# Attention and spectral mix on one core: other cuts of q over the DMA engines

## The chip, the core and the metric

The kernel runs on one core of a Trainium2 chip. A core has TensorE (PE; its weight loads are shown apart, as PEld), VectorE (DVE), ScalarE (ACT), GpSimd (POOL) and SyncE (SP). Sixteen DMA engines move data between memory (HBM) and the core's own memory of 128 partitions. POOL and SP issue the transfers; POOL's go through queue 0 and change float32 into bfloat16 on the way, SP's through queue 1.

The metric is the time of one execution on the device in microseconds (us), the median of several runs.

## The reference

Sliding-window causal attention over 8 batches, 8 heads, 576 positions and 64 channels, then a mix in the frequency domain with one complex 512 x 512 matrix for each of 64 modes, then a channel product:

```python
def _attn_ref(q, k, v):                     # q, k, v: (8, 8, 576, 64) float32
    scores = scale * np.matmul(q, k.transpose(0, 1, 3, 2))
    mask = (rel >= 0) & (rel < 64)          # rel = query position - key position
    ...
    return np.matmul(attn, v)

def _moe_ref(x, w_r, w_i, w_ch):            # x: (8, 576, 512), the heads side by side
    X = np.fft.rfft(x, axis=1)              # w_r, w_i: (64, 512, 512), w_ch: (512, 512)
    Yr = einsum("bmd,mde->bme", Xr, w_r) - einsum("bmd,mde->bme", Xi, w_i)
    Yi = einsum("bmd,mde->bme", Xr, w_i) + einsum("bmd,mde->bme", Xi, w_r)
    Y[:, :n_modes] = Yr + 1j * Yi
    u = x + np.fft.irfft(Y, n=S, axis=1)
    return u + np.maximum(u @ w_ch, 0.0)
```

Most of the bytes are weights: 127 matrices of 512 x 512 float32 (w_i of mode 0 isn't needed) make 133 of the 162.5 MB that are read.

## The kernel before, in words

**Stages.** Lines 465 to 543 are attention. Batch by batch, PE transposes k, v and q (`transpose_units`, line 275, with the transposes at line 289), forms the scores in windows of 512 columns (line 361), ACT takes the exponential (line 367), PE multiplies with v (line 385), DVE normalises into `x_sb` (line 393), and PE does the forward transform (line 407). The next stage, lines 947 to 976, runs over the 127 weights in a fixed order: `half` (line 652) multiplies one weight with the transformed rows (line 660), `issue` (line 609) starts the loads of later weights as places come free, and pieces of the channel product and the inverse transform are set between them. The end (from line 1039) has the products that need the last modes, and writes the output through SP (lines 1031 and 1034).

**Loads.** POOL issues, in the order of the program, q, k and v of each batch (`load`, line 137) and the weights (`load_w`, line 177, one of 512 KB in bfloat16; `load_two`, line 182, two in one transfer). The order of PE and POOL is written out by hand (`manual_schedule`); DVE's and ACT's is not in the attention stage. `refill` (line 444) is called after each unit of transposes: once k of batch b has been transposed, it loads k of batch b + 2 into the same buffer (two buffers of each kind, `rawp`) and then, from batch 1 on, one weight (`early`, line 428); the same with v and q. So the loads of batch 5 are issued while batch 3 is in work, those of batch 7 while batch 5 is.

Each transfer of POOL ends on one of eight semaphores, which go round: the ninth transfer waits until the first has landed on all its engines.

**How rows go to DMA engines.** A tensor of a batch is 128 partitions by two halves (heads 0 to 3 and 4 to 7) of 18 x 64 values, 2304 bytes in bfloat16. Transferred whole (line 152) it gives each of the sixteen engines 16 such rows. Three loads of q, those of batches 5, 6 and 7, are cut by `UNEVEN` (line 113). An entry is (n, m, columns, small one behind): the first n x m partitions of the lower half are read as n groups interleaved (line 143, outer dimension n), which puts them on n engines alone, m rows on each. These are n engines in turn, from where the last such transfer stopped; for the entry with 17, one engine. The upper half (line 145) goes over all sixteen, 8 rows each. What is left of the lower half (line 148: 3, 72 and 94 rows) goes in equal parts from engine 0 on. `step_on` (line 131) issues a small transfer of 2n rows of 32 bytes that nobody reads: it moves the turn on by n engines. The assertion of line 116 keeps the sum of all turns a multiple of 16.

| batch | turn | rows of the cut, each | small one behind |
| --- | --- | --- | --- |
| 5 | engines 0 to 4 | 25 | 5, 6 |
| 6 | engines 7, 8 | 28 | 9 to 14 |
| 7 | engine 15 | 34 | none |

**The order is undone in the transposes.** The interleaved rows stand in other partitions. `back` (line 121) makes for each cut a permuted identity (two DVE copies, lines 126 and 127), and `part` (line 283) takes it in place of `ident_bf` for the half that was cut (line 291).

Of the kernel before, what the change touches and what calls it, by code (L numbers as in the profile page):

```python
# [11 lines left out]
BF16 = mybir.dt.bfloat16  # L12
# [8 lines left out]
def view(ap, off, dims):  # L21

    return bass.AP(ap.tensor, ap.offset + off, [list(ap.ap[0])] + [list(d) for d in dims])
# [3 lines left out]
def kernel(  # L27
# [10 lines left out]
    nc = tc.nc  # L38
    B, H, S, D = q.shape
# [8 lines left out]
    RUN = S // 32  # L48
# [6 lines left out]
    def evac(o, i, on_act):  # L55

        if on_act:
            return nc.scalar.copy(out=o, in_=i)  # L58
        return nc.vector.tensor_copy(out=o, in_=i)  # L59
# [10 lines left out]
    ident_bf = consts.tile([128, 128], BF16, name="ident_bf")  # L70
# [19 lines left out]
    acons = p1.enter_context(tc.tile_pool(name="acons", bufs=1, side="right"))  # L90
# [10 lines left out]
    RAW = {"k": k, "q": q, "v": v}  # L101

    def raw_tile(which):
        return rawp.tile([128, 2, RUN * D], BF16, name="r" + which)

    def runs(b, which):
        return RAW[which][b].rearrange("(x g) (p c) d -> (g p) x (c d)", g=4, c=RUN)
# [1 line left out]

    UNEVEN = {(5, "q"): (5, 25, RUN, 2), (6, "q"): (2, 28, RUN, 6), (7, "q"): (17, 2, RUN, 0)}
    for lot in UNEVEN.values():
        assert lot[0] <= 16 or all(lot[0] % d for d in range(2, 17))
    assert sum((n if n <= 16 else 1) + x for n, m, c, x in UNEVEN.values()) % 16 == 0
    aside = [acons.tile([34, 16], BF16, name=f"aside{i}") for i in range(len(UNEVEN))]
    forms = {lot[:2]: acons.tile([128, 128], BF16, name=f"back{lot[0]}") for lot in UNEVEN.values()}
    made = set()

    def back(key):

        n, m = form = UNEVEN[key][:2]
        if form not in made:
            made.add(form)
            nc.vector.tensor_copy(out=forms[form], in_=ident_bf)
            nc.vector.tensor_copy(out=view(forms[form], 0, [[1, n], [n, m]]),
                                  in_=view(ident_bf, 0, [[m, n], [1, m]]))
        return forms[form]

    def step_on(key, n):

        n, src = (n if n > 1 else 17), k[0, :H // 2].rearrange("g (p c) d -> (g p) (c d)", c=RUN)
        nc.gpsimd.dma_start(out=aside[list(UNEVEN).index(key)][:2 * n],
                            in_=src[:2 * n, 0:16].rearrange("(r a) c -> a r c", a=n))

    def load(b, which):
        r = raw_tile(which)
        if (b, which) in UNEVEN:
            lower, upper = [RAW[which][b, x * H // 2:(x + 1) * H // 2].rearrange("g (p c) d -> (g p) (c d)", c=RUN)  # L140
                            for x in range(2)]
            n, m, c, behind = UNEVEN[b, which]
            cut = lower[:n * m].rearrange("(r a) c -> a r c", a=n)
            nc.gpsimd.dma_start(out=r[:n * m, 0, :c * D], in_=cut[:, :, :c * D])
            nc.gpsimd.dma_start(out=r[:, 1, :], in_=upper)
            if c < RUN:
                nc.gpsimd.dma_start(out=r[:, 0, c * D:], in_=lower[:, c * D:])
            nc.gpsimd.dma_start(out=r[n * m:, 0, :c * D], in_=lower[n * m:, :c * D])
            if behind:
                step_on((b, which), behind)  # L150
        else:
            nc.gpsimd.dma_start(out=r, in_=runs(b, which))
        raws[b, which] = r
# [65 lines left out]
    with tc.manual_schedule(engines=ALL_FOUR):  # L219
# [3 lines left out]
        with tc.tile_pool(name="tmpf", bufs=1, side="right") as tmp:  # L223
            mo = tmp.tile([128, NM], FP32, name="mo")
            to = tmp.tile([128, NT], FP32, name="to")
            nc.gpsimd.iota(mo, pattern=[[1, NM]], base=0, channel_multiplier=0,
                           allow_small_or_imprecise_dtypes=True)
            nc.gpsimd.iota(to, pattern=[[128, NT]], base=0, channel_multiplier=1,
                           allow_small_or_imprecise_dtypes=True)
            nc.gpsimd.memset(ident, 0.0)  # L230
            nc.gpsimd.affine_select(out=ident, in_=ident, compare_op=ALU.not_equal, fill=1.0,
                                    base=0, pattern=[[-1, 128]], channel_multiplier=1)
            load(0, "q")
            load(0, "v")
            for t0, t1 in ((0, 3), (3, NT)):
                n = t1 - t0
                mt = tmp.tile([128, 2, n * NM], FP32, name="mtf")
                nc.vector.tensor_tensor(out=view(mt, 0, [[NM, n], [1, NM]]), in0=view(mo, 0, [[0, n], [1, NM]]),
                                        in1=view(to, t0, [[1, n], [0, NM]]), op=ALU.mult)
                gen_trig(tmp, mt, n * NM, trigF[:, t0:t1, 0:NM], trigF[:, t0:t1, NM:2 * NM], "f")  # L240
                if t0 == 0:
                    nc.vector.tensor_copy(out=ident_bf, in_=ident)
        nc.scalar.activation(out=spark, in_=ident[:, 0:1], func=ACT_F.Exp)
        raws[0, "k"] = raw_tile("k")
        for c, engine in enumerate((nc.vector, nc.gpsimd, nc.vector)):
            cc = slice(6 * D * c, 6 * D * (c + 1))
            engine.tensor_copy(out=raws[0, "k"][:, :, cc], in_=k_first[:, :, cc])
        load(1, "k")
        for i in range(4):
            half = i % 2  # L250
# [24 lines left out]
    def transpose_units(b):  # L275

        rk, rq, rv = (raws.pop((b, which)) for which in "kqv")
        qT = qtp.tile([128, 4, S], BF16, name="qT")
        vT = vtp.tile([128, 4, S], BF16, name="vT")
        kT, vt = kTs[b % 2], vts[b % 2]  # L280
        qTs[b] = qT

        def part(src, dst, c0, on_act, which):
            def f():
                turned = UNEVEN.get((b, which), (0, 0, 0))[2]
                ps = ps_misc.tile([128, 6, 128], BF16, name="pst", tag="misc")
                for c in range(6):
                    for hh in range(2):
                        nc.tensor.transpose(out=ps[64 * hh:64 * hh + 64, c, :],  # L289
                                            in_=src[:, hh, (c0 + c) * D:(c0 + c + 1) * D],  # L290
                                            identity=back((b, which)) if hh == 0 and c0 + c < turned else ident_bf)
                evac(view(dst, c0, [[S, 4], [RUN, 32], [1, 6]]),
                     view(ps, 0, [[32, 4], [1, 32], [128, 6]]), on_act)
            return f

        def vback(u):
            def f():
                ps = ps_misc.tile([128, 6, 128], BF16, name="psv", tag="misc")
                for i in range(6):
                    a, j = divmod(6 * u + i, 9)  # L300
                    if j == 4:
                        parts = [(0, 64, 2 * a, 512), (64, 64, 2 * a + 1, 0)]
                    else:
                        parts = [(0, 128, 2 * a + (j > 4), 128 * j - (j > 4) * S)]
                    for r0, n, g, t0 in parts:
                        nc.tensor.transpose(out=ps[r0:r0 + n, i, :],  # L306
                                            in_=vT[:, g, t0:t0 + n], identity=ident_bf)
                evac(view(vt, 6 * u * VW, [[18 * VW, 2], [VW, 6], [1, D]]),
                     view(ps, 0, [[D, 2], [128, 6], [1, D]]), u != 1)
                if u:  # L310
                    hs = slice(u - 1, u + 2, 2)
                    nc.vector.tensor_copy(out=vt[64:128, 1, hs, 1:9], in_=vt[64:128, 0, hs, 0:8])
                    nc.vector.tensor_copy(out=vt[0:64, 1, hs], in_=vt[0:64, 0, hs])
            return f

        return [*(part(rk, kT, 6 * i, i != 1, "k") for i in range(3)),
                *(part(rv, vT, 6 * i, i == 1, "v") for i in range(3)),
                *(part(rq, qT, 6 * i, i != 1, "q") for i in range(3)),
                vback(0), vback(1), vback(2)]
# [50 lines left out]
    def closes(w):  # L370

        return min(-(-8 * w // 9) * 9 or 9, 8 * w + 8)
# [115 lines left out]
    with tc.manual_schedule(engines={E.PE, E.Pool}):  # L488
# [16 lines left out]
        for w in range(NWIN + 1):  # L505
# [5 lines left out]
            n = len(todo)  # L511
            if 0 < w < NWIN:
                scores(w)
            if w:
                cut = closes(w - 1)
# [12 lines left out]
            if w in (NWIN - 4, NWIN - 1):  # L528
                i = (B - 2) % 2 if w == NWIN - 4 else (B - 1) % 2
                spare(kTs[i])  # L530
                spare(qtp.tile([128, 4, S], BF16, name="qT"))
            if w in (NWIN - 4, NWIN):
                i = (B - 2) % 2 if w == NWIN - 4 else (B - 1) % 2
# [386 lines left out]
    for k, (f, delta, n, few) in enumerate(items):  # L920
        i = S_I + k * (T_I - 2 - S_I) // len(items)
# [25 lines left out]
    with tc.manual_schedule(engines=ALL_FOUR):  # L947
# [92 lines left out]
        for k in range(6):  # L1040
# [10 lines left out]
                              in_=view(psys[0], 0, [[2 * B, NC], [2, B], [1, 2]]))  # L1051
# [78 lines left out]
```

## Time and profile before

Three runs: 423.84, 423.85 and 424.44 us; median 423.85.

| what | us |
| --- | --- |
| the profiled execution | 424.01 |
| its span, first to last instruction | 422.2 |
| PE busy | 350.5 |
| DVE busy | 189.9 |
| ACT busy | 159.9 |
| POOL busy | 86.5 |
| mean granted clock of TensorE | 0.859 of full |

HBM is read at 162.53 MB and written at 9.44 MB. The page gives bytes of a transfer as they arrive: 92.55 MB over 31312 packets, since POOL's loads halve the bytes. In the page's rows a line such as `wt<-in_moe_w_i_dram POOLq DMA_DIRECT2D x19, 512.0 KB, 15.8` tells of 19 transfers of 512 KB that took 15.8 us (median) from issue to landing. In a timeline the columns are start, duration, engine, line, operation and tiles, number merged, and in brackets the idle time before it with what ended it.

### The profile page before, as it was taken

Reading aid. Unit: us, or ns where it says so; the run is one execution under the profiler, and the core shown is the slowest. Engines: PE = TensorE matmul, PEld = TensorE weight load, DVE = VectorE, ACT = ScalarE, POOL = GpSimd, SP = SyncE. Lnnn points to the kernel's source line nnn. Section 1 sums busy time; section 2 is a strip of 40 time slices with the busy share of each in tenths; the row PEclk is TensorE's granted clock in tenths of the full one; section 3 lists DMA queues with packets and bytes.
Section 4 is the critical chain, followed back from the end, with each engine's and each line's share of the span. In section 5 each row is a group of like instructions: output and inputs, shape, how many; then the busy total and the mean of one; then the engine's idle time right before and its main releaser. Section 6 shows DMA issues by size and latency. Waiting matters only on the chain.

```text
span 422.2 us, 11483 instructions
## 1 busy us (share of the span) xinstructions
PE 350.5 (83%) x5185; PEld 230.8 (55%) x5185; DVE 189.9 (45%) x365; ACT 159.9 (38%) x267; POOL 86.5 (20%) x154
## 2 busy tenths in 40 slices
PE   7899999999988779954768576767699999998994
PEld 3466666656654566743546454545456565554441
DVE  6576776676764100634343251211114344340895
ACT  5666865766765100122102110200023343330863
POOL 6231232341221220411112011210121212300000
PEclk9999999999999655978668665667579999999998
DMA  8999999999999999999999999999999999997598
GB/s 211 212 213 213 214 212 209 213 209 209 213 215 213 213 214 262 214 214 215 214 213 215 213 215 213 215 214 214 214 214 215 213 214 213 214 215 144 208 371 318
DMA packets 31312, 92.55 MB, mean 219 GB/s; under 512 B 3744, under 2 KB 3744, under 8 KB 31264
## 3 DMA queue, kind: packets, MB, share of 16 engines
q0 software_dynamic: 26016, 81.21, 96.5%
q1 hardware_dynamic: 5248, 10.62, 6.9%
q8 instruction: 40, 0.66, 0.6%
q14 instruction: 8, 0.07, 0.0%
HBM read 162.53 MB, written 9.44 MB: 407 GB/s over the span
## 4 chain that ended last, share of the span: by engine, by line
DMA 44%; PE 40%; DVE 7%; issue 3%; ACT 2%; DVEq 0%; POOLq 0%; ACTq 0%
DMA wms<-in_moe_w_i_dram 23%; DMA wms<-in_moe_w_r_dram 22%; PE psy L660 6%; PE pso L385 6%; PE pst L289 5%; PE psv L306 3%; PE psx L407 3%; PE pss L1005 3%; DVE x_sb L393 2%; PE pss L998 2%; PE pss L342 2%; PE pss L361 2%; PE psz L801 2%; PE psy L945 2%; DVE vT L59 1%
## 5 line engine op out<-in xcount | busy, mean ns | idle before, releaser
L801 PE MATMUL psz<-wch,xT 128*128 128x512 f32 x144 | 59.2, 548 | 0.0
L795 DVE CAST xT<-pxt 128x1024 fp32r<-128x1024 bf16 x18 | 22.0, 1224 | 78.5 <-PE pxt L790 78.5
L804 ACT CAST Z<-psz 128x1024 fp32r<-128x1024 f32 x18 | 18.2, 1012 | 99.0 <-PE psz L801 99.0
L367 ACT ACTIVATE et<-pss 128x512 bf16<-128x512 f32 x72 | 39.2, 600 | 13.6 <-PE pss L361 13.6
L660 PE MATMUL psy<-XQ,wls 128*128 128x16 bf16 x560 | 21.9, 192 | 23.8 <-DMA wls<-in_moe_w_r_dram 15.1
L660 PE MATMUL psy<-XQ,wms 128*128 128x16 bf16 x624 | 25.1, 192 | 19.9 <-DMA wms<-in_moe_w_i_dram 13.8
L660 PEld LDWEIGHTS <-wms 128*128 128x128 bf16 x624 | 21.4, 102 | 31.9 <-DMA wms<-in_moe_w_i_dram 16.7
L660 PEld LDWEIGHTS <-wls 128*128 128x128 bf16 x560 | 19.3, 104 | 33.4 <-DMA wls<-in_moe_w_r_dram 18.2
L801 PEld LDWEIGHTS psz<-wch,xT 128*128 128x128 f32 x144 | 33.8, 261 | 5.2
L385 PE MATMUL pso<-vt,et 128*64 128x65 bf16 (+1 forms) x576 | 32.3, 203 | 4.3 <-DVE x_sb L393 1.9
L853 DVE TENSOR_TENSOR Z<-pse,Z 128x1024 fp32r<-128x1024 f32 x16 | 19.6, 1225 | 29.7 <-PE pse L842 29.7
L385 PEld LDWEIGHTS <-et 128*64 128x64 bf16 (+1 forms) x576 | 22.2, 109 | 15.1 <-issue 7.7
L660 PE MATMUL psy<-XQ,wt 128*128 128x16 bf16 x560 | 20.9, 192 | 7.1 <-issue 3.0
L393 DVE TENSOR_TENSOR x_sb<-pso,rcp 128x640 bf16<-128x640 f32 x32 | 26.3, 822 | 0.9
L660 PEld LDWEIGHTS <-wt 128*128 128x128 bf16 x560 | 18.5, 105 | 11.7 <-DMA wt<-in_moe_w_i_dram 4.5
L59 DVE COPY vT<-pst 128x768 bf16<-128x768 bf16 x16 | 15.3, 958 | 13.1 <-PE pst L289 11.6
L1023 ACT ACTIVATE pss<-pss 128x512 f32<-128x512 f32 x35 | 18.5, 581 | 4.8 <-PE pss L1005 4.2
L59 DVE CAST YT<-psy 128x256 fp32r<-128x256 f32 x6 | 2.5, 424 | 38.6 <-PE psy L660 29.6
L945 PE MATMUL psy<-trigF,ident_bf 128*128 128x512 bf16 x46 | 17.6, 447 | 0.1
L58 ACT COPY vt<-psv 128x768 bf16<-128x768 bf16 x16 | 12.9, 809 | 8.3 <-PE psv L306 8.2
L306 PE MATMUL psv<-ident_bf,vT 128*128 128x128 bf16 (+1 forms) x160 | 15.5, 226 | 0.6 <-DVE vT L59 0.6
L342 PE MATMUL pss<-band,ident_bf 64*64 64x512 bf16 x120 | 15.9, 397 | 0.0
(198 smaller groups left out, 621.8 us busy)
## 6 DMA issues: line engine op xcount, KB each, us to landing
wt<-in_moe_w_i_dram POOLq DMA_DIRECT2D x19, 512.0 KB, 15.8
wt<-in_moe_w_r_dram POOLq DMA_DIRECT2D x16, 512.0 KB, 16.7
wls<-in_moe_w_r_dram POOLq DMA_DIRECT2D x8, 1024.0 KB, 21.6
wms<-in_moe_w_i_dram POOLq DMA_DIRECT2D x7, 1024.0 KB, 21.2
wms<-in_moe_w_r_dram POOLq DMA_DIRECT2D x7, 1024.0 KB, 21.2
wls<-in_moe_w_i_dram POOLq DMA_DIRECT2D x6, 1024.0 KB, 21.6
rv<-in_v_dram POOLq DMA_DIRECT2D x8, 576.0 KB, 12.8
rk<-in_k_dram POOLq DMA_DIRECT2D x7, 576.0 KB, 12.4
```

Of the source, the lines that this page charges most:

```text
L59: return nc.vector.tensor_copy(out=o, in_=i)
L289: nc.tensor.transpose(out=ps[64 * hh:64 * hh + 64, c, :], in_=src[:, hh, (c0 + c) * D:(c0 + c + 1) * D], identity=back((b, which)) if hh = ...
L306: nc.tensor.transpose(out=ps[r0:r0 + n, i, :], in_=vT[:, g, t0:t0 + n], identity=ident_bf)
L342: nc.tensor.matmul(out=pss[(2 * w + hh) % 3][64 * half:64 * half + 64, :], lhsT=ident_bf[pp, pp], rhs=view(band[pp], 128 * half, [[0, WIN ...
L367: nc.scalar.activation(out=et[:, hh, :], in_=pss[(2 * w + hh) % 3], func=ACT_F.Exp, scale=EX_SCALE)
L385: nc.tensor.matmul(out=pso[po, hh, block(b, i // 2) * VW:block(b, i // 2) * VW + D + 1], lhsT=et[pk, hh, col:col + 64], rhs=vt[pk, 1 - f % ...
L393: nc.vector.tensor_tensor(out=view(x_sb, b * NT * DM + g * D, [[4 * D, 2], [DM, NT], [1, D]]), in0=view(pso, 0, [[512, 2], [VW, NT], [1, D]]),
L660: nc.tensor.matmul(out=view(psy, off + 2 * B * e, [[1, 2 * B]]), lhsT=w[:, c, 128 * e:128 * e + 128], rhs=XQ[:, m // HM, c, :, 1 - im:3 - ...
L795: nc.vector.tensor_copy(out=o, in_=i)
L801: nc.tensor.matmul(out=psz[s][:, j, :], lhsT=xts[s % 2][0][:, j, 128 * c:128 * c + 128], rhs=wch[:, c, :], start=(c == 0), stop=(c == NC - 1))
L853: nc.vector.tensor_tensor(out=z, in0=ps, in1=z, op=ALU.add)
L945: nc.tensor.matmul(out=o, lhsT=ident_bf, rhs=view(trigF, 0, [[1, DM]]), start=True, stop=True)
```

## The change

It concerns the loads of k and q of batches 5, 6 and 7. The eight engines that get more rows than the others are the same: 0 to 4, 7, 8 and 15.

- q of batch 5 is cut with (2, 32, 1): 64 partitions of the lower half as two groups of 32, then the upper half over all sixteen engines, then the other 64 partitions of the lower half.
- q of batch 6 is cut with (6, 16, 2): 96 partitions of the lower half as six groups of 16, a small transfer for ten engines, 96 partitions of the upper half as six groups of 16, then the last 32 partitions of both halves.
- q of batch 7 is loaded whole.
- Small transfers (`lead_on`) for 7, 6 and 11 engines are issued ahead of k of batches 5, 6 and 7 (`STEPS`); none follow q.
- `back` is built for two cuts where there were three, and `part` takes it for as many halves as were cut.

The turns are then:

| before | transfer | engines | rows each |
| --- | --- | --- | --- |
| k of 5 | small, 7 | 0 to 6 | small |
| in q of 5 | cut of 2 | 7, 8 | 32 |
| k of 6 | small, 6 | 9 to 14 | small |
| in q of 6 | cut of 6 | 15, 0 to 4 | 16 |
| in q of 6 | small, 10 | 5 to 14 | small |
| in q of 6 | cut of 6 | 15, 0 to 4 | 16 |
| k of 7 | small, 11 | 5 to 15 | small |

POOL issues 131 transfers before and after.

```diff
-    UNEVEN = {(5, "q"): (5, 25, RUN, 2), (6, "q"): (2, 28, RUN, 6), (7, "q"): (17, 2, RUN, 0)}
...
-    aside = [acons.tile([34, 16], BF16, name=f"aside{i}") for i in range(len(UNEVEN))]
+    UNEVEN = {(5, "q"): (2, 32, 1), (6, "q"): (6, 16, 2)}
+    STEPS = {(5, "k"): 7, (6, "k"): 6, (7, "k"): 11}
+    assert (sum(STEPS.values()) + sum((n, n + 16)[i - 1] for n, m, i in UNEVEN.values())) % 16 == 0
...
-    def step_on(key, n):
-
-        n, src = (n if n > 1 else 17), k[0, :H // 2].rearrange("g (p c) d -> (g p) (c d)", c=RUN)
-        nc.gpsimd.dma_start(out=aside[list(UNEVEN).index(key)][:2 * n],
-                            in_=src[:2 * n, 0:16].rearrange("(r a) c -> a r c", a=n))
+    def raw_rows(b, which, x):
+        return RAW[which][b, x * H // 2:(x + 1) * H // 2].rearrange("g (p c) d -> (g p) (c d)", c=RUN)
+
+    def lead_on(n):
+        aside = acons.tile([2 * n, 16], BF16, name=f"aside{n}")
+        nc.gpsimd.dma_start(out=aside, in_=raw_rows(0, "k", 0)[:2 * n, 0:16].rearrange("(r a) c -> a r c", a=n))

     def load(b, which):
+        if (b, which) in STEPS:
+            lead_on(STEPS[b, which])
         r = raw_tile(which)
         if (b, which) in UNEVEN:
...
-            n, m, c, behind = UNEVEN[b, which]
-            cut = lower[:n * m].rearrange("(r a) c -> a r c", a=n)
-            nc.gpsimd.dma_start(out=r[:n * m, 0, :c * D], in_=cut[:, :, :c * D])
-            nc.gpsimd.dma_start(out=r[:, 1, :], in_=upper)
-            if c < RUN:
-                nc.gpsimd.dma_start(out=r[:, 0, c * D:], in_=lower[:, c * D:])
-            nc.gpsimd.dma_start(out=r[n * m:, 0, :c * D], in_=lower[n * m:, :c * D])
-            if behind:
-                step_on((b, which), behind)
+            n, m, halves = UNEVEN[b, which]
+            for x in range(halves):
+                nc.gpsimd.dma_start(out=r[:n * m, x, :],
+                                    in_=raw_rows(b, which, x)[:n * m].rearrange("(r a) c -> a r c", a=n))
+                if x + 1 < halves:
+                    lead_on(16 - n)
+            if halves == 1:
+                nc.gpsimd.dma_start(out=r[:, 1, :], in_=raw_rows(b, which, 1))
+                nc.gpsimd.dma_start(out=r[n * m:, 0, :], in_=raw_rows(b, which, 0)[n * m:])
+            else:
+                nc.gpsimd.dma_start(out=r[n * m:], in_=runs(b, which)[n * m:])
         else:
             nc.gpsimd.dma_start(out=r, in_=runs(b, which))
...
-                turned = UNEVEN.get((b, which), (0, 0, 0))[2]
+                n, m, halves = UNEVEN.get((b, which), (0, 0, 0))
...
-                                            identity=back((b, which)) if hh == 0 and c0 + c < turned else ident_bf)
+                                            identity=back((n, m)) if hh < halves else ident_bf)
```

More of the change, by code (lines that the diff above doesn't have):

```diff
@@ L107, in runs, with back @@
         return RAW[which][b].rearrange("(x g) (p c) d -> (g p) x (c d)", g=4, c=RUN)
-    UNEVEN = {(5, "q"): (5, 25, RUN, 2), (6, "q"): (2, 28, RUN, 6), (7, "q"): (17, 2, RUN, 0)}
-    for lot in UNEVEN.values():
-        assert lot[0] <= 16 or all(lot[0] % d for d in range(2, 17))
-    assert sum((n if n <= 16 else 1) + x for n, m, c, x in UNEVEN.values()) % 16 == 0
-    aside = [acons.tile([34, 16], BF16, name=f"aside{i}") for i in range(len(UNEVEN))]
+    UNEVEN = {(5, "q"): (2, 32, 1), (6, "q"): (6, 16, 2)}
+    STEPS = {(5, "k"): 7, (6, "k"): 6, (7, "k"): 11}
+    assert (sum(STEPS.values()) + sum((n, n + 16)[i - 1] for n, m, i in UNEVEN.values())) % 16 == 0
     forms = {lot[:2]: acons.tile([128, 128], BF16, name=f"back{lot[0]}") for lot in UNEVEN.values()}
     made = set()
-    def back(key):
-        n, m = form = UNEVEN[key][:2]
+    def back(form):
+        n, m = form
         if form not in made:
@@ L129, in back @@
         return forms[form]
-    def step_on(key, n):
-        n, src = (n if n > 1 else 17), k[0, :H // 2].rearrange("g (p c) d -> (g p) (c d)", c=RUN)
-        nc.gpsimd.dma_start(out=aside[list(UNEVEN).index(key)][:2 * n],
-                            in_=src[:2 * n, 0:16].rearrange("(r a) c -> a r c", a=n))
+    def raw_rows(b, which, x):
[3 more added lines that the diff above has]
+        nc.gpsimd.dma_start(out=aside, in_=raw_rows(0, "k", 0)[:2 * n, 0:16].rearrange("(r a) c -> a r c", a=n))
     def load(b, which):
+        if (b, which) in STEPS:
+            lead_on(STEPS[b, which])
         r = raw_tile(which)
         if (b, which) in UNEVEN:
-            lower, upper = [RAW[which][b, x * H // 2:(x + 1) * H // 2].rearrange("g (p c) d -> (g p) (c d)", c=RUN)
-                            for x in range(2)]
-            n, m, c, behind = UNEVEN[b, which]
-            cut = lower[:n * m].rearrange("(r a) c -> a r c", a=n)
-            nc.gpsimd.dma_start(out=r[:n * m, 0, :c * D], in_=cut[:, :, :c * D])
-            nc.gpsimd.dma_start(out=r[:, 1, :], in_=upper)
-            if c < RUN:
-                nc.gpsimd.dma_start(out=r[:, 0, c * D:], in_=lower[:, c * D:])
-            nc.gpsimd.dma_start(out=r[n * m:, 0, :c * D], in_=lower[n * m:, :c * D])
-            if behind:
-                step_on((b, which), behind)
+            n, m, halves = UNEVEN[b, which]
[9 more added lines that the diff above has]
+                nc.gpsimd.dma_start(out=r[n * m:], in_=runs(b, which)[n * m:])
         else:
```

## The prediction

> **What bounds the kernel now.** First the page: the 40 slices of DMA, the table of queues, and the head of the chain of waits.
>
> ```profile
> DMA  8999999999999999999999999999999999997598
> ...
> DMA packets 31312, 92.55 MB, mean 219 GB/s; under 512 B 3744, under 2 KB 3744, under 8 KB 31264
> ...
> q0 software_dynamic: 26016, 81.21, 96.5%
> ...
> q8 instruction: 40, 0.66, 0.6%
> ...
> DMA 44%; PE 40%; DVE 7%; issue 3%; ACT 2%; DVEq 0%; POOLq 0%; ACTq 0%
> DMA wms<-in_moe_w_i_dram 23%; DMA wms<-in_moe_w_r_dram 22%; PE psy L660 6%; PE pso L385 6%; PE pst L289 5%; PE psv L306 3%; PE psx L407 3%; PE pss L1005 3%; DVE x_sb L393 2%; PE pss L998 2%; PE pss L342 2%; PE pss L361 2%; PE psz L801 2%; PE psy L945 2%; DVE vT L59 1%
> ```
>
> The sixteen DMA engines are at 9 in every slice up to the last weight, and the longest links of the chain are weights (wms). Next the timeline of PE where the last weight lands:
>
> ```profile
> 386.27 0.65 PE L660 MATMUL psy<-XQ,wt 128*128 128x16 bf16 x16 [0.56 <-DMA wt<-in_moe_w_r_dram]
> 386.75 1.68 PE L945 MATMUL pss<-trigF,ident_bf 128*128 128x512 bf16 x7
> 388.76 0.65 PE L660 MATMUL psy<-XQ,wms 128*128 128x16 bf16 x16 [0.33 <-DMA wms<-in_moe_w_i_dram]
> ```
>
> PE waits for each of the last weights, and what follows 388.76 (two products, relu, output) takes 422.2 - 388.8 = 33.4 us whatever came before. So the end is the last landing plus 33.4 us, and a transfer has landed when the slowest of sixteen engines has. The trace keeps sixteen landings for each transfer that POOL issues. For the last weight they lie, in us after the first of them, at 0, 0.36, 0.69, 0.82, 0.87, 0.90, 1.20, 1.26, 1.40, 1.44, 1.47, 1.69, 1.84, 1.86, 2.05, 2.31: mean 1.26, so an even share would end 1.05 us sooner. None of the engines stands idle before: adding up, from the packet records, each packet's step to the next one on its engine gives 16 engines full (0.98 to 1.02 in every 5 us from 10 to 385). What an engine ends late by is therefore its own work.
>
> Two kinds of work differ between them. A row of q is 2304 bytes; at 213 GB/s over 16 engines (the window 5 to 55 us) it takes 2304 / 13.3 = 0.173 us. And the 40 instruction packets take 0.6% of 16 x 422.2 us, 1.01 us each; their durations repeat with period eight (974, 961, 893, 893, 948, 945, 935, 974 ns), so they go round eight engines, four or five each, 4.0 to 5.1 us. The other eight get the extra rows. Counting rows by the cut of L137 to L150: engines 0 to 2 get 381, 3 and 4 380, 7 and 8 383, 15 382; the fetching ones (5, 6, 9 to 13) 355, and 14 352. That is 25 to 28 rows, 4.3 to 4.8 us, against up to 5.1 us of fetching, and by this sum the fetching engines end later. An engine that a cut leaves out gets a 4-byte packet for each row of an engine that takes part; in the records these follow each other at 0.006 us. By the cut they number 1248: 131 transfers x 16 end packets + 1248 + 16 + 384 of SP's queue = 3744, the page's count under 512 B.
>
> **The change, term by term.**
> Rows and small packets, from the new cut (extra turns at engines 7 and 8, then twice at 15 and 0 to 4): 384 rows on each of the eight, 352 on each other; 828 four-byte packets, 68 of 32 bytes (0.024 us each). Fetching engines: -3 x 0.173 - 24 x 0.006 + 4 x 0.024 = -0.56 us (engine 14, -0.06). Engines 0 to 2: +0.40; 3 and 4: +0.57; 7 and 8: +0.10; 15: +0.24. The latest fetching engine goes from 2.31 to 1.75; the eight others, which the sums put in the lower part of the list (to about 1.3), reach 1.6 to 1.8. Last landing: **-0.55 us**.
>
> Issues on POOL: 131 before and after. Eight semaphores go round, so a transfer waits until the one eight places back has landed on its slowest engine; lines of POOL's timeline:
>
> ```profile
> 79.32 0.83 POOL L134 DMA_DIRECT2D aside<-in_k_dram  x1 [0.49 <-DMA wt<-in_moe_w_r_dram]
> 82.15 0.56 POOL L179 DMA_DIRECT2D wt<-in_moe_w_r_dram  x1 [2.00 <-DMA rk<-in_k_dram]
> 84.87 0.72 POOL L152 DMA_DIRECT2D rk<-in_k_dram  x1 [2.16 <-PE pst L289]
> 87.39 0.55 POOL L179 DMA_DIRECT2D wt<-in_moe_w_r_dram  x1 [1.80 <-DMA rv<-in_v_dram]
> 90.08 0.71 POOL L152 DMA_DIRECT2D rv<-in_v_dram  x1 [2.14 <-DMA wt<-in_moe_w_i_dram]
> ```
>
> A small transfer fills a place of the eight and gives next to no work, so here the cover of the fastest engine is thinnest. For k of batch 7 at 84.87: seven transfers stand between (v 2.78, two weights 2.46 each, the pieces of q and the small one 0.19 + 1.40 + 0.05 + 0.03) = 9.4 us, less the 4.9 us by which the slowest engine is behind the fastest, less 0.6 (0.3 to the landing, 0.3 to the issue) = 3.9 us of work left; the trace has 4.1 from this issue to the fastest engine's landing of the transfer ahead, 3.8 without the 0.3. The sum holds.
>
> After, k of batch 7 waits for v of batch 6. Between stand two weights, two cuts of six, two leads and the rest of q: 2.46 + 0.12 + 0.03 + 0.12 + 0.71 + 2.46 + 0.05 = 5.95 us for a fetching engine. Engines 7 and 8 are behind it by 32 x 0.173 - 32 x 0.006 = 5.3, less one fetch, 4.3 us. Left: 5.95 - 4.3 - 0.6 = **1.0 us** against 3.9. All other issues of these turns keep over 2 us. How long a new transfer takes from issue to its first packet no row shows bare. From below: the issuing instruction, 0.72 us. From above: q of batch 0 is issued at 1.60, and queue 0 has no packet before 5.2 us, so 3.6 us (the engines were busy with k until then). I take 1.4: POOL's 0.72 plus what SP's first transfer shows, 0.65 from the end of its issue (1.17) to its first packet (1.82). The gap is then 1.4 - 1.0 = 0.4 us (0 to 2.6 at the ends) on the three or four fetching engines that are furthest ahead; later work never gives it back. That is about half of the fetching engines; whether the latest is one of them is open, so I charge half a gap and a little, **+0.25 us**.
>
> The Trainium skill ("DMA: Bandwidth & Descriptors", Latency and other measured facts) puts a first byte at about 1 us on POOL's path against 0.6 us on SP's. The second agrees with the 0.65 us here; the first would make the 1.4 into 1.7 and the gap 0.7 us, and the sum would end at -0.15 instead of -0.3.
>
> Nothing else lies on the path. Two DVE copies fewer (0.19 and 0.37 us) end before DVE's own wait of 0.71 us for k at 5.95; without that cover 0.5 us of a start that the full DMA engines don't see. Transposes with a permuted identity are 54 before and after, 219 ns both ways. Transfers land early: k, v, q of batch 7 land at 97 to 108 and are read from 109.3 on, so 1 us more is hidden; uncovered, it would be 1 us.
>
> **Sum:** -0.55 + 0.25 = -0.3 us. The profiled execution (424.01 around a span of 422.2) would be 423.7; it lies 0.16 above the median, so the forecast is **423.55** on 423.85. About 0.2%, 0.85 us, is what a measurement can tell.
>
> **Rivals.**
> *The cover runs out.* If issue to first packet takes 3.0 to 3.6 us, all fetching engines that are ahead stand still for 2.0 to 2.6 us before k of batch 7, and the latest of them end 1.45 to 2.05 us later than 1.75 less what their place in the list saves (0.5): -0.55 + 2.0 - 0.5 = +0.95 up to +1.55, 424.8 to 425.4. It decides from 2.9 us on. For: 3.6 us is what the first transfer shows. Against: queue 0 follows on k's last packet at once on every engine (5.21 to 5.57), so it had been waiting.
>
> *A nearly even finish.* No gap, and the late ends happen to be those that lose rows: to the mean, -1.05 - 0.16 (420 four-byte packets fewer over 16 engines) = -1.2 at the most, 422.65 to 423.0. Against: the terms of the eight others.
>
> *The late engines are those that get more.* Then 2.31 turns into 2.31 + 0.4: 424.2. Against: the sums of rows and fetches.
>
> *The turns miss their engines.* Steps of 7, 2, 6, 6, 10, 6, 11 add to 48, three rounds of 16, so every launch begins alike; were one counted otherwise, fetching engines would get the 32 rows: 5.5 + 5.1 us, 429 and more. Against: the old steps (5, 2, 2, 6, 1) are counted the same way and give the spread above.
>
> *Confined transfers hold up the rest.* Cuts are 25, 28 and 34 rows deep before, 32, 16 and 16 after: 23 rows x 0.173 = 4.0 us less if the other engines stood still meanwhile, 419.9. Against: nobody stands idle. The Trainium skill (same page, Rules for kernel authors) speaks against an outermost dimension under 16 at all, since it confines a transfer to so many engines; here the others run on.
>
> **How the numbers follow.** Forecast 0.52 (423.2 to 423.75); cover runs out 0.20 (0.18 past +0.85); nearly even 0.15 (0.12 past -0.85); late ones get more 0.08; missed engines 0.03; confined 0.02. Faster by over 0.2%: 0.12 + 0.02 = 0.14; slower: 0.18 + 0.03 = 0.21; same 0.65. The range goes from 422.9 to 425.3 and leaves out the last two cases and the tails of the second and third.
>
> **What would show it.** Packets under 512 B 3376 (2096 + 828 + 68 + 384), all packets 30944, queue 0 25648. PE's wait for the last weight ends near 388.4. The idle step, if any, stands in the DMA share between 88 and 92 us (1.09 before), with POOL's issue of rk near 88.5. A last landing spread over 2.3 us, or a dip there of more than 1 us, would make the forecast wrong.

## The result, and the profile after

| | before | after |
| --- | --- | --- |
| median, us | 423.86 (7 runs) | 425.42 (7 runs) |
| lowest to highest | 423.82 to 424.44 | 424.94 to 427.04 |
| the profiled execution | 424.01 | 424.94 |
| its span | 422.2 | 423.2 |
| wait for the last weight ends | 388.76 | 389.71 |

The changed kernel takes 1.0039 of the time before (95% interval 1.0025 to 1.0053), 1.56 us more. The forecast was 0.3 us less, with a range up to 425.3. A second set of seven runs of the same kernel gave 425.89 us (ratio 1.0061, 1.0036 to 1.0085). The profiled execution after is the fastest of its seven, so the profile shows less of the loss than the median.

The page of the changed kernel; the digits and the GB/s are those of 40 slices of 10.6 us:

```profile
DMA  8999999999999999999999999999999999997598
GB/s 212 211 213 214 212 213 209 213 193 212 215 214 213 215 213 264 212 215 213 215 215 213 215 214 214 215 215 213 215 214 215 213 214 213 215 212 141 206 371 317
DMA packets 30944, 92.55 MB, mean 219 GB/s; under 512 B 3376, under 2 KB 3376, under 8 KB 30896
...
q0 software_dynamic: 25648, 81.21, 96.3%
...
q8 instruction: 40, 0.66, 0.6%
q14 instruction: 8, 0.07, 0.0%
...
PE 44%; DMA 40%; DVE 7%; ACT 3%; issue 2%; DVEq 0%; POOLq 0%; ACTq 0%
```

The three packet counts are those forecast, so the cuts and the small transfers do what the diff says, and DMA still holds 40% of the chain of waits. The digits of busy time show nothing: 9 before, in and behind the place in question. The bytes do: the ninth slice (84.6 to 95.2 us) moved 193 GB/s, all others up to the last weight 209 or more. The windows narrow it down. Of each line the last two columns are the DMA share and GB/s; first before, then after:

```profile
85.00:90.00 5.00, 4.92 (x99) 3.24 (x96) 3.81 (x8) 4.17 (x10) 1.13 (x2) 1.00 1.11 206
90.00:95.00 5.00, 4.45 (x64) 2.44 (x64) 3.33 (x7) 2.50 (x5) 3.54 (x6) 1.00 1.09 212
```

```profile
85.00:90.00 5.00, 4.92 (x114) 3.33 (x110) 3.81 (x8) 4.17 (x9) 1.29 (x2) 1.00 1.08 203
90.00:95.00 5.00, 4.50 (x62) 2.41 (x60) 3.90 (x8) 2.92 (x5) 3.17 (x6) 1.00 1.05 182
95.00:100.00 5.00, 4.92 (x116) 3.36 (x115) 2.59 (x6) 3.05 (x6) 1.50 (x3) 1.00 1.09 211
```

Between 90 and 95 us 182 GB/s went through where 212 had; the busy share fell only from 1.09 to 1.05, since it adds up the times of packets, and a packet that takes long counts as busy for all of that time. POOL's timeline of the changed kernel there:

```profile
83.53 0.57 POOL L179 DMA_DIRECT2D wt<-in_moe_w_r_dram  x1 [1.62 <-DMA rk<-in_k_dram]
86.00 0.56 POOL L133 DMA_DIRECT2D aside<-in_k_dram  x1 [1.89 <-DMA wt<-in_moe_w_i_dram]
89.01 0.74 POOL L152 DMA_DIRECT2D rk<-in_k_dram  x1 [2.46 <-PE pss L361]
91.25 0.55 POOL L179 DMA_DIRECT2D wt<-in_moe_w_r_dram  x1 [1.51 <-DMA rq<-in_q_dram]
```

k of batch 7 (rk) is issued at 89.01. The releaser named (PE, L361) is only the semaphore that came last by the profile. What k needs from PE are the transposes of k of batch 5, which free its buffer, and they ended at 81.2. What came late is v of batch 6, eight transfers back, whose sixteenth landing is at 88.46; the 0.55 us from there to the issue are as long as in the kernel before (84.31 to 84.87). On PE the delay has become a later last weight and nothing else:

```profile
389.71 0.65 PE L660 MATMUL psy<-XQ,wms 128*128 128x16 bf16 x16 [0.27 <-DMA wms<-in_moe_w_i_dram]
```

389.71 is 0.95 us after the 388.76 of before, and the two profiled executions are 0.93 us apart.

**What happened on the engines.** The records don't name a DMA engine. Which engines are meant is told here by the count of turns and rows: of the sixteen landings of a transfer, the eight early ones are taken as those of the fetching engines, which have fewer rows. The landings of one transfer are matched with those of the next in their order. The small transfer ahead of k lands on the eight fetching engines between 90.22 and 91.75 us, on the others between 94.34 and 94.83. k, issued 1.21 us ahead of that 90.22 (this is the cover: the time for which the fastest engine still has work), lands 2.56 to 2.65 us after it on the eight slow ones, and at 94.63 to 94.98 on the fetching ones, all eight almost together. Against 2.61 us they have lost 0.6 to 1.8 us each, 1.23 on average. Two things make that up. Counting open packets every 0.01 us from 84 to 98 us, engines without any add to an estimated 3.6 engine-us (before: 0.1). This is an estimate because packets on one engine overlap a little, so that some 17.5 are open when all sixteen engines work; the bare count of what is missing to sixteen is 1.9 (before: 0). And of k's first packets, from 90.47 us on, nine took 594, 688, 754, 952, 781, 932, 674, 775 and 689 ns where a packet of 2304 bytes takes 192; over this window slow packets took 8.7 engine-us too long (before: 0.5). Together that is 12.3 / 16 = 0.77 us on each engine.

The same sums for all kernels that follow; "mean" and "last" are those of the sixteen landings of the last weight, from one profiled execution each. Two executions of one kernel can differ here by a few tenths of a us, the changed kernel's last landing by 1.3. The last two columns are estimates, good for telling a standstill from none: by the bare count the four kernels with a standstill have 1.9, 2.8, 22.5 and 4.5, in the order of the table, and all others at most 0.05.

| kernel | mean, us | last, us | no packet open, engine-us | slow packets, engine-us |
| --- | --- | --- | --- | --- |
| before | 387.66 | 388.71 | 0.1 | 0.5 |
| after | 388.31 | 389.66 | 3.6 | 8.7 |
| after, again | 388.54 | 390.95 | 5.8 | 6.3 |
| small 11 behind q of 7 | 387.42 | 388.75 | 0.0 | 0.5 |
| small 11 ahead of v of 7 | 387.88 | 389.08 | 0.0 | 1.0 |
| one more small one | 390.15 | 392.95 | 26.6 | 8.9 |
| before, two small ones | 388.61 | 390.95 | 7.0 | 5.5 |
| threes, 11 behind | 387.75, 388.06 | 388.80, 389.10 | 0.0, 0.0 | 1.5, 3.9 |
| threes, 11 ahead | 388.44, 388.05 | 389.56, 389.50 | 0.0, 0.1 | 14.4, 5.4 |
| second cut 16 on 2 to 4 | 387.78 | 388.97 | 0.0 | 0.5 |
| first cut 16 on 15, 0, 1 | 387.71 | 389.54 | 0.0 | 1.8 |
| second cut 28 on 2 to 4 | 387.83 | 388.73 | 0.0 | 0.7 |

### The profile page after: what moved, and what is told of

Read it like the earlier page. It is cut to its first block, busy times and chain, and to the rows that moved or that the text cites. A ratio compares the mean times of both kernels' runs of the same rounds, so it can differ in the third digit from the quotient of the medians.

```text
span 423.2 us, 11481 instructions
## 1 busy us (share of the span) xinstructions
PE 354.2 (84%) x5185; PEld 233.6 (55%) x5185; DVE 189.8 (45%) x363; ACT 160.0 (38%) x267; POOL 86.2 (20%) x154
## 4 chain that ended last, share of the span: by engine, by line
PE 44%; DMA 40%; DVE 7%; ACT 3%; issue 2%; DVEq 0%; POOLq 0%; ACTq 0%
DMA wls<-in_moe_w_r_dram 20%; DMA wls<-in_moe_w_i_dram 10%; PE psy L660 7%; DMA wms<-in_moe_w_i_dram 6%; PE pso L385 6%; PE pst L289 5%; DMA wms<-in_moe_w_r_dram 3%; PE psv L306 3%; PE psx L407 3%; PE pss L1005 3%; DVE x_sb L393 2%; PE pss L998 2%; PE pss L342 2%; PE pss L361 2%; PE psy L945 2%
## 5 line engine op out<-in xcount | busy, mean ns | idle before, releaser
L801 PE MATMUL psz<-wch,xT 128*128 128x512 f32 x144 | 60.6, 560 | 0.0
L801 PEld LDWEIGHTS psz<-wch,xT 128*128 128x128 f32 x144 | 34.9, 268 | 5.4
```

The lines of the kernel that those rows point to most:

```text
L801: nc.tensor.matmul(out=psz[s][:, j, :], lhsT=xts[s % 2][0][:, j, 128 * c:128 * c + 128], rhs=wch[:, c, :], start=(c == 0), stop=(c == NC - 1))
```

## The experiments

Each time stands beside the kernel before in the same job (medians 423.85 to 423.97).

**The small transfer for eleven, moved away from k of batch 7.** Rows and turns stay as in the change; k of 7 then waits for the transfer one place earlier, and has a full weight ahead of it. The first kernel has the small transfer behind q of batch 7, the second ahead of v.

```diff
-    STEPS = {(5, "k"): 7, (6, "k"): 6, (7, "k"): 11}
+    STEPS = {(5, "k"): 7, (6, "k"): 6}
+    BEHIND = {(7, "q"): 11}
...
+        if (b, which) in BEHIND:
+            lead_on(BEHIND[b, which])
```

> As the changed kernel, with the small transfer for 11 engines moved from ahead of k of batch 7 to behind q of batch 7; the same 131 transfers, the same rows on each engine. Theory 1 (the cover runs out at the issue of k of batch 7): that issue comes about 2.5 us earlier, against the transfer one place earlier; 8.7 - 4.3 - 0.6 = 3.8 us of work are then left on the fetching engines; no dip in the DMA share at 90 us (1.09), the landings of k of batch 7 spread over about 5.5 us again, the last weight lands near 388.2 us, time 423.3 (423.0 to 423.7). Theory 2 (the new shares of rows are the worse ones): unchanged, 425.4. Theory 3 (the number of small packets and transfers costs): unchanged, 425.4.

```diff
-    STEPS = {(5, "k"): 7, (6, "k"): 6, (7, "k"): 11}
+    STEPS = {(5, "k"): 7, (6, "k"): 6, (7, "v"): 11}
```

> As the changed kernel, with the small transfer for 11 engines two places later only, ahead of v of batch 7 instead of k. Theory 1: the place is what counts; at k of batch 7 3.8 us of work are left, at v of batch 7 about 3.4; no dip, 423.3 (423.0 to 423.8). Theories 2 and 3: 425.4.

Measured: 424.05 us (ratio 1.0005, 0.9996 to 1.0014) behind q, 424.12 (1.0003, 0.9994 to 1.0012) ahead of v. POOL's timeline, the window from 90 to 95 us, and PE's line of the last weight, of the first:

```profile
85.97 0.72 POOL L153 DMA_DIRECT2D rk<-in_k_dram  x1 [2.13 <-PE pso L388]
88.58 0.55 POOL L182 DMA_DIRECT2D wt<-in_moe_w_r_dram  x1 [1.89 <-DMA rv<-in_v_dram]
```

```profile
90.00:95.00 5.00, 4.53 (x62) 2.42 (x60) 3.85 (x8) 2.95 (x5) 3.10 (x5) 1.00 1.09 212
```

```profile
388.80 0.65 PE L663 MATMUL psy<-XQ,wms 128*128 128x16 bf16 x16 [0.29 <-DMA wms<-in_moe_w_i_dram]
```

Both kernels miss the 423.3 that was expected of the place as the cause, which counted on the new rows to gain, but nearly all of the 1.56 us is gone. k is issued at 85.97, 3.70 us ahead of the fastest engine's landing of the transfer before it, its landings follow those of that transfer by 2.78 us on all sixteen engines within 0.1 us, and the window 90 to 95 us is back at 212 GB/s. So the place of this one small transfer costs 425.42 - 424.05 = 1.4 us (1.8 by the second set of runs); in the profiles the mean landing of the last weight moves by 0.89 us and the last one by 0.91. What is left of the change, its other shares of rows, gains nothing: 388.75 against 388.71 before. Whether the mean fell, as the 0.16 us reckoned from 420 small packets fewer would have it, these profiles don't show: it is 0.24 us earlier than before in the first kernel and 0.22 later in the second, which has the same rows. In both the last engine is further behind the mean (1.33 and 1.20 us, before 1.05), and alone: the second last is 0.72 and 0.61 us ahead of it.

**More small transfers ahead of k of batch 7.** If thin cover is the cause, one neutral place more (32 rows of 32 bytes over all engines) must make it worse by a calculable amount, and two such places must bring the loss into the kernel before, whose rows are untouched. The first edit is of the changed kernel, the second of the kernel before.

```diff
+        if (b, which) == (7, "k"):
+            nc.gpsimd.dma_start(out=acons.tile([32, 16], BF16, name="asideN"), in_=raw_rows(0, "k", 0)[:32, 0:16])
```

> As the changed kernel, with one more small transfer (32 rows of 32 bytes over all sixteen engines, so that the turns stay) between the one for 11 engines and k of batch 7. Theory 1: the issue of k then waits for the weight behind v of batch 6, 2.5 us more, and nothing is left to cover it; the fetching engines stand still about 2.4 us longer, time 427.2 to 428.2, issue of k of batch 7 near 91.5 us. Theories 2 and 3: 425.4 to 425.5.

```diff
+        if (b, which) == (7, "k"):
+            src = k[0, :H // 2].rearrange("g (p c) d -> (g p) (c d)", c=RUN)
+            for i in range(2):
+                nc.gpsimd.dma_start(out=acons.tile([32, 16], BF16, name=f"asideN{i}"), in_=src[:32, 0:16])
```

> The kernel before, with two such small transfers ahead of k of batch 7; its cuts and shares of rows stay. Theory 1: the issue of k waits two places further on, near 89.9 us instead of 84.9, and of the 3.9 us of work left there about nothing stays; engine 15 and four or five fetching engines stand still for 1 to 3 us, time 425.0 to 426.3. Theories 2 and 3: 423.9 to 424.0.

Measured: 428.01 us (ratio 1.0107, 1.0074 to 1.014) and 426.36 (1.0054, 1.004 to 1.0067), the first inside Theory 1's range and the second just above it. POOL's timelines, first of the changed kernel with one more, then of the kernel before with two:

```profile
86.57 0.56 POOL L133 DMA_DIRECT2D aside<-in_k_dram  x1 [1.88 <-DMA wt<-in_moe_w_i_dram]
89.50 0.49 POOL L139 DMA_DIRECT2D asideN<-in_k_dram  x1 [2.37 <-DMA rv<-in_v_dram]
92.33 0.74 POOL L154 DMA_DIRECT2D rk<-in_k_dram  x1 [2.33 <-PE psv L308]
```

```profile
84.61 0.51 POOL L141 DMA_DIRECT2D asideN<-in_k_dram  x1 [1.92 <-DMA wt<-in_moe_w_i_dram]
87.34 0.49 POOL L141 DMA_DIRECT2D asideN<-in_k_dram  x1 [2.22 <-DMA rv<-in_v_dram]
90.12 0.74 POOL L156 DMA_DIRECT2D rk<-in_k_dram  x1 [2.29 <-PE pst L293]
```

Each small transfer takes a place of the eight, and POOL waits 1.9 to 2.4 us for one, so the next issue moves by about 3 us: 85.97, 89.01, 92.33 for none, one and two small ones between. The fastest engine's landing of the transfer ahead then comes 3.70 us and 1.21 us after the issue of k, and 1.15 us before it. Engines without a packet: 0, 3.6 and 26.6 engine-us. The kernel before loses 2.5 us in the same way, with every row as it was. The thin cover is shown as the cause of the loss. In both kernels the restart looks as in the changed kernel: the first slow packets of k start 1.45 and 1.44 us after its issue (at 93.78 and 91.56) and take 927 and 918 ns. Here the standstill is long enough for the busy share to show it too:

```profile
90.00:95.00 5.00, 4.46 (x63) 2.34 (x60) 3.48 (x8) 2.84 (x5) 2.67 (x5) 1.00 0.73 119
```

This is the window of the changed kernel with one more.

**Other cuts, and the late engine.** Two cuts of three engines with 32 rows each (one of each half) need no small transfer for ten between them, and give every engine the rows that the change gives it. `load`, `back` and `part` take a list of cuts for this; that part of the edit is left out here.

```diff
-    UNEVEN = {(5, "q"): (2, 32, 1), (6, "q"): (6, 16, 2)}
-    STEPS = {(5, "k"): 7, (6, "k"): 6, (7, "k"): 11}
+    UNEVEN = {(5, "q"): ((2, 32),), (6, "q"): ((3, 32), (3, 32))}
+    STEPS = {(5, "k"): 7, (6, "k"): 6}
+    BEHIND = {(7, "q"): 11}
...
```

> As e1_lead11_last, with q of batch 6 in two cuts of three engines, 32 rows each (lower half on 15, 0, 1, upper half on 2, 3, 4), in place of two cuts of six with 16 rows; the small transfer for 10 engines between them falls away. Rows on each engine as in the changed kernel; 130 transfers. Theory 1 (the cover is what counts, and there is enough of it): as e1, 424.05 (423.85 to 424.25), no dip near 90 us. If depth of a cut cost time by itself (32 rows in place of 16): over 424.5. In the last landings one engine should again end alone, some 0.7 us behind the next one.

Measured: 424.46 us (ratio 1.0008, 0.999 to 1.0025). k is issued 6.24 us ahead, and no engine is without a packet; still it is above the 424.25 to which the expectation went, just under the 424.5 from which depth of a cut was to be blamed. One engine is alone at the end here too (0.45 us behind the second). To tell which kind of engine that is, three row-taking engines got fewer rows, and the others made up for it: once 2, 3 and 4 (second cut 16 rows), once 15, 0 and 1 (first cut 16, that is (3, 16), (3, 32)).

```diff
-    UNEVEN = {(5, "q"): ((2, 32),), (6, "q"): ((3, 32), (3, 32))}
+    UNEVEN = {(5, "q"): ((2, 32),), (6, "q"): ((3, 32), (3, 16))}
```

> As e5, with 16 rows in place of 32 in the second cut: engines 2, 3 and 4 get 371 rows (13 fewer, -2.2 us), the thirteen others 3 more each (+0.5 us). Theory R (the last engine of e1 is one of those that take rows, held up by instruction packets of 8192 bytes that fall on it): if it is 2, 3 or 4, no engine ends alone any more, the last landings spread over about 2.3 us, time 423.9; if it is 15, 0 or 1, it ends 0.5 us later, 424.55. Theory F (the last engine is one of the fetching ones): 424.55 here and in e7 alike.

> The mirror of e6: engines 15, 0 and 1 get 371 rows, the others 3 more. Theory R: 423.9 if the last engine is 15, 0 or 1, 424.55 if it is 2, 3 or 4; just one of e6 and e7 loses the engine that ends alone. Theory F: 424.55 in both.

Measured: 423.82 us (ratio 0.9991, 0.9973 to 1.0009) and 424.66 (1.001, 0.9992 to 1.0028). The intervals don't part them from the kernel before, but the times part them from each other: ten runs from 423.57 to 424.22 and ten from 424.37 to 425.06. That is what Theory R forecast if the last engine is 2, 3 or 4 (423.9 and 424.55), and not what Theory F forecast (424.55 in both). The landings of the last weight, in us after the first, agree:

```
16 on 2, 3, 4    0  1.35  1.59  2.23  2.62  ...  3.53  3.88
16 on 15, 0, 1   0  0.36  0.70  2.10  ...  3.26  3.63  4.34
```

With 2 to 4 relieved the last engine is 0.35 us behind the second; with 15, 0 and 1 relieved it is 0.71 behind. So with the threes the lone late engine is one of 2, 3 and 4, which got more rows, and none of those that fetch. For the sixes, which give the same rows, this is inferred and not shown, and who was last in the kernel before no run tells. The first three landings (0 to 1.59, 0 to 0.70) are by the sum the relieved engines, whose share is too small by now; so a smaller relief was tried:

```diff
-    UNEVEN = {(5, "q"): ((2, 32),), (6, "q"): ((3, 32), (3, 32))}
+    UNEVEN = {(5, "q"): ((2, 32),), (6, "q"): ((3, 32), (3, 28))}
```

> As e5, with 28 rows in place of 32 in the second cut (84 partitions; the 44 others go 3 each to engines 0 to 13 and 2 to engine 14): engines 2, 3 and 4 get 3 rows fewer (-0.5 us), engines 0, 1 and 5 to 13 one more (+0.2 us), engine 15 two fewer. Theory R (the last engine is among 2, 3 and 4, by two 8192-byte instruction packets): the engine that ends alone comes 0.5 us sooner and the rest 0.2 us later, all within about 2.0 us; 0.3 to 0.5 us under e1 and e5, 423.6 to 423.9, about the time before. Theory F (a fetching engine): 0.2 us over e5.

Measured: 423.89 us (ratio 0.9997, 0.9988 to 1.0006), 0.57 us under the 424.46 of the kernel with 32 rows (in another job; the kernel before has 423.97 and 423.96 in the two). Since the cuts are still 32, 32 and 28 rows deep, depth by itself is hardly what made that one slower. The last landing stands 0.90 us behind the mean, the least of all kernels here, and it comes at 388.73: what the order of the landings gains is not a measurable gain in time over the kernel before. No kernel here is shown faster than that one.

**Is it the place of the small transfer, or the thin cover?** Threes without the small one for ten leave one place more: the small transfer for eleven can stand ahead of k of batch 7, where the change has it, and k is issued 5.60 us ahead all the same.

```diff
-    STEPS = {(5, "k"): 7, (6, "k"): 6}
-    BEHIND = {(7, "q"): 11}
+    STEPS = {(5, "k"): 7, (6, "k"): 6, (7, "k"): 11}
```

> As e5, with the small transfer for 11 engines ahead of k of batch 7 again, where the changed kernel has it; only the small one for 10 engines is gone, since the cuts of three need none. Theory 1: k of batch 7 again waits for the weight ahead of v of batch 6, 3.5 to 4 us of work are left on the fetching engines, no dip near 90 us, 424.0 to 424.5 as e5. If the small transfer ahead of k did harm by itself, whatever stands among the eight: 425.4.

Measured: 424.56 us (ratio 1.0014, 1.0005 to 1.0023), as the threes with it behind, and 0.9 under the change, though the small transfer stands where the change has it:

```profile
83.47 0.56 POOL L134 DMA_DIRECT2D aside<-in_k_dram  x1 [1.66 <-DMA rk<-in_k_dram]
86.17 0.73 POOL L152 DMA_DIRECT2D rk<-in_k_dram  x1 [2.14 <-PE pxq L417]
```

So it is the cover that counts. No engine was without a packet. The profiled execution (424.86) was a surprise, though. Its windows:

```profile
85.00:90.00 5.00, 4.92 (x113) 3.38 (x111) 3.88 (x8) 4.18 (x9) 1.27 (x2) 1.00 1.13 193
90.00:95.00 5.00, 4.46 (x63) 2.35 (x60) 3.48 (x8) 2.85 (x5) 2.06 (x4) 1.00 1.13 187
```

The GB/s fall to 187 as in the changed kernel, but here the busy share rises (1.13): all engines have packets and these are slow, about 14 engine-us too long, of q, of a weight and of k. So slow packets need no standstill, and the ones of the changed kernel could have been a matter of chance. Three kernels were therefore run once more, unaltered.

> The changed kernel once more, unaltered. In its first profile three or four engines had no packet open between 89.75 and 90.5 us (some 2 engine-us), and fourteen packets of k of batch 7 between 90.4 and 92.0 us took 6.0 us more in sum than such packets do. If the standstill makes its first packets slow, both are there again: open engines down to 12 near 90.2 us, slow packets of 5 to 8 us in sum, last landing 389.5 to 389.9, median 425.0 to 425.6. If the slow packets were a spell of slow memory in one execution, they are gone, and the last landing is near 389.0.

> The kernel with two cuts of three engines and the small transfer for eleven ahead of k of batch 7 once more, unaltered. Its first profile had no engine without a packet, and yet 14.8 us of slow packets in sum between 87 and 92 us. If that was a spell in one execution, it is gone, or stands at another place: slow packets under 2 us in sum from 80 to 100 us, last landing 388.8 to 389.0, median 424.2 to 424.6. If this order of transfers makes it, the spell is at 87 to 92 us again with 10 us or more, and the last landing near 389.5.

> The same with the small transfer for eleven behind q of batch 7, once more, unaltered: no slow spell in its first profile (1.8 us in sum from 80 to 100 us, as the kernel before has 0.6). If spells come by chance, this kernel can have one too, anywhere; if the order of transfers makes them, it has none, and its median is 424.2 to 424.6 as e11's or up to 0.3 us below it.

Measured: 425.89 us (ratio 1.0061, 1.0036 to 1.0085), 424.79 (1.0019, 1.0011 to 1.0028) and 424.69 (1.0018, 1.0009 to 1.0027). The windows of the first and the second:

```profile
90.00:95.00 5.00, 4.17 (x61) 2.22 (x61) 3.59 (x7) 2.11 (x4) 3.14 (x6) 1.00 1.02 180
```

```profile
90.00:95.00 5.00, 4.46 (x85) 2.48 (x86) 3.01 (x7) 1.79 (x3) 1.93 (x3) 1.00 1.12 195
```

In the changed kernel everything is there again: k issued 0.81 us ahead, 5.8 engine-us without a packet, first packets of k up to 1038 ns, the fetching engines 1.0 to 2.1 us late, all eight landing between 94.87 and 95.62. (That the last landing is as late as 390.95 has a second reason: one engine 1.28 us behind the second, which no run here explains.) In the threes with the small one ahead the slow packets shrink from 14.4 to 5.4 engine-us, and with it behind they grow from 1.5 to 3.9. So with threes slow packets near 90 us come in varying number, wherever the small transfer stands; this neither confirms nor kills the idea that their order makes them. With sixes they were there in all three executions with a standstill (8.7, 6.3 and, with one more small transfer, 8.9) and in neither of the two without (0.5, 1.0); the kernel before has them too once it has a standstill (5.5 against 0.5). What makes a packet slow is not settled. Of the 0.4 and 0.6 us by which 424.46 and 424.69 lie above the 424.05 of the sixes, slow packets would make 1.5 / 16 = 0.1 and 3.9 / 16 = 0.2 us; the rest is open.

## Why the prediction was wrong

**What bounds the kernel, and where an effect would show: right.** The last landing plus a fixed tail: 423.2 - 389.7 = 33.5 us against 33.4. Packet counts, the order of the turns, 131 issues, and a loss of bytes at this place alone: as forecast. The sign against the forecast that I had named came as well: the last landing is spread over 2.51 us, more than 2.3.

**"Left: 1.0 us against 3.9": right.** The profile has 1.21 us from the issue of k to the fastest engine's landing, 0.9 without the 0.3 for the landing itself. Its place (POOL's issue near 88.5; it is 89.01) and the dip between 88 and 92 us were named.

**"I take 1.4" for issue to first packet: right.** It is 90.47 - 89.01 = 1.46 us. The 1.7 that I had estimated from about 1 us on POOL's path in the Trainium skill ("DMA: Bandwidth & Descriptors", Latency and other measured facts) is further off than the 1.4: here 0.72 us passed from the end of the issuing instruction to the first packet. Neither sum would have come near the result.

**"Half a gap and a little, +0.25 us": the step that failed first.** It was measured at 1.4 us in the medians, 1.8 by the second set of runs (0.9 in the profiles, of which the changed kernel's is its fastest execution). I counted a gap as over when the first packet starts. But the first packets took 0.6 to 0.95 us instead of 0.19, and all eight fetching engines landed k late, also those whose transfer ahead landed only at 91.3 to 91.8 and that I had covered. So the loss is not 0.4 us on three or four engines but 0.6 to 1.8 us on eight. And I discounted a loss by half because the latest engine might not be among those that stand: yet with it the engines come out in another order, and mean and last moved alike (0.89 and 0.91 us against the kernel with the small transfer moved).

**"Last landing: -0.55 us": the step that failed second.** By the two kernels that have the change's rows and no standstill it is +0.2 us (0.9996 to 1.0014, and 0.9994 to 1.0012; -0.55 us would be 0.9987). Wrong was who ends last. I put the fetching engines last, and so relieved them by 3 rows; the experiments with 16 rows put the last engine of the new shares, cut in threes, among 2, 3 and 4, to which the sum added 0.40 to 0.57 us. That is the rival of the late engines that get more, 424.2 (chance 0.08), and the kernels without the standstill are at 424.05 and 424.12. My own figures hardly gave the order on which the term rests: 1.01 us for a fetch came from the rounded 0.6%, while the eight durations beside it have a mean of 0.94. Five fetches are then 4.5 to 4.9 us, and not 5.1, against 4.3 to 4.8 us of rows. Another thing left out of the sum was the queue of eight further instruction packets on the page (q14, 8192 bytes, 322 ns each). Linking each engine's landings back from the last weight puts the four of them after 115 us on row-taking engines, two on the one that ends last, 0.6 us; this is a reading of the records, no kernel tested it.

The two steps together make up the miss: 1.4 instead of 0.25, and +0.2 instead of -0.55, are 1.9 us; the result lies 1.86 us from the forecast.

**The rival that came true** is the one in which the cover runs out (424.8 to 425.4, chance 0.20): the place is its place. Its condition is not: it asked for 2.9 us or more from issue to first packet, and 1.46 us was measured, 2.1 to 2.4 us to the end of a first packet. That the time, 425.42, lies at its upper edge is luck: it has a standstill of 2.0 to 2.6 us, where the engines lost 0.6 to 1.8, and it sets off against that the 0.55 us of gain that didn't come.

## What to carry to other kernels

Where transfers end on a few rotating semaphores, a tiny transfer costs a full place: work out, at every issue near it, how much the fastest engine still has, and keep some 3 us there (here a cover of 1.2 us cost 1.4 us of time, and 3.3 to 3.7 us cost nothing that could be measured; what lies between wasn't tried). Count a restart by when the first packets end, not by when they start. And before loads are shifted between engines, find out by taking load off some of them which one ends last; a sum whose terms differ by less than their own rounding, or that leaves out half a microsecond of other packets, can point at the wrong ones.

## What the runs showed of the hardware

- After a standstill the first packet of a transfer came 1.46 us after POOL began to issue it (1.45 and 1.44 us to the first slow one in the two kernels with more small transfers), and nine of its first packets of 2304 bytes took 594 to 952 ns instead of 192 (again nine, 598 to 1038 ns, in the second profile).
- Packets can also be slow with all engines at work: in one execution some 85 packets between 84 and 98 us took about 14 engine-us too long, and from 90 to 95 us the busy share was 1.13 where the kernel before has 1.09, while the GB/s were 187 against 212. So the busy share alone didn't show the time lost here; only a long standstill brought it down clearly (0.73, with 119 GB/s).
- A small transfer, which lands on an engine about 0.2 us after the one ahead of it, moved the next issue on POOL by about 3 us (85.97, 89.01, 92.33), because its place came free only when its predecessor had landed on the slowest engine.
